# Moving the second softmax's transposes two slots earlier and rewriting TensorE's order in an attention and gated feed-forward kernel

## The chip, the cores and the metric

The kernel runs on one core of one Trainium2 chip. The metric is device time in microseconds. The times before are those of three runs; beside them stands one profiled execution, whose trace gives every duration in this document.

The engines go by the profile's names: PE is TensorE's matmul, PEld its weight load, DVE is VectorE, ACT is ScalarE, POOL is GpSimd, and SP is SyncE, which here only issues DMAs. SPq, POOLq and ACTq are the queues in which those engines issue DMAs, in program order.

## The reference

Four sequences x of 12416 rows by 128 go through an attention with 32 inducing points, and its result, 49664 rows by 128, through a gated feed-forward layer of width 1536:

```
def mab(q, kv):
    s = scale * (q @ kv.transpose(0, 2, 1))
    s = s - s.max(-1, keepdims=True)
    a = np.exp(s)
    a /= a.sum(-1, keepdims=True) + 1e-09
    return a @ kv
h = mab(I, x)                   # first softmax: 32 rows, each over 12416
y = mab(x, h)                   # second softmax: 12416 rows, each over 32
gate = 1.0 / (1.0 + np.exp(-(y @ w_gate)))
val = y @ w_val
out = gate * val @ w_out
```

## The kernel before

**The work.** A sequence is 97 chunks of 128 rows: six groups of 16 chunks and a single one. The attention result y is never formed. Since y = a2 h, the products h w_gate and h w_val (32 by 1536) are formed once for each sequence (tile `hwt`), and the feed-forward layer starts from the normalised weights a2 of the second softmax, transposed, in tiles `a2r`. A block is four chunks, 512 rows, by 12 slices of the width; a slice of a block is called a chunk of work below, as in the code. For each of them TensorE fills a gate bank (`g_ps`, 32 x 128 weights, 512 columns), ScalarE takes its tanh into a ring of 16 places (`issue_gate`, L1164), TensorE fills a value bank (`v_ps` or `vm_ps`, L1121), VectorE forms u = (tanh + 1) * v (`product`, L1351), and TensorE adds four 128 x 128 products of u with w_out into `acc_ps` (`out_mm`, L1250). After a block, ScalarE evacuates `acc_ps` into one of three buffers `o32` (L1275), and SP stores it (L1276).

**Beside it.** While the feed-forward layer of sequence b runs, the next sequence's first softmax (stage 1) and the second softmax of coming groups (stage 2) run in the gaps. `plan_stage2` lays out a group of stage 2: scores on TensorE (L651), copied by ScalarE (L688), row maxima by a tree on POOL (L698 to L703), the exponential on ScalarE (L712, the step called `weigh`), the row sums on POOL (L720 to L726), the reciprocal and the normalised weights `a2n` on POOL (L744 to L766), and last `turn`: SP issues a DMA that transposes `a2n` into one of three buffers `a2r` (L777). `plan_stage1` does the like for a group of the first softmax: scores (L368), a maximum on VectorE (L380), an exponential on ScalarE (L393), a transposing DMA on SP (`turn_dma`, L417), and sums on TensorE (L428). `x_transpose_dma` (L174) issues the transposes of x itself on SP.

**What sets the order.** The program writes each engine's instructions in one fixed order. Two things set it. The string `ORDER` is TensorE's order, written out by hand or by a planner beforehand: `g` fills a gate bank, `V` or `W` fills a value bank, `x` is VectorE's product, `o12` is twelve of the output products, and `p`, `a` and `d` let a waiting side step run on TensorE, ScalarE or VectorE. Value banks come in pairs, first `v2` with two chunks of work, then `vm` with one; after a `W` the second one has two as well, so a pair takes 3 or 4 chunks.

The second thing is the agenda. Every plan gives its steps a slot, and a slot is three chunks of work, counted from the beginning of the sequence (`position`); a sequence has 96. Before each fill of `v2`, `turn_page` takes the steps that have come due. A step marked "do" is issued at once, on whatever engine it uses; the others wait for their letter in `ORDER`. So the slot of `turn` decides where the transpose of `a2n` stands in SP's queue among the stores, the stage-1 transposes and the transposes of x. The exponential's slot is `weigh`, the sums come at weigh + 1, the normalising at weigh + 3, and `turn` at weigh + 8; it is weigh + 7 where the group takes the single chunk along (`far`), and weigh + 5 for the very first group (`soon`).

Of the kernel before, what the change touches and what calls it, by code (L numbers as in the profile page):

```python
# [54 lines left out]
NEXT = "the slot behind"  # L55
RING = 16
ORDER = """
ggVxgpgVxpVxgVd0xgo12gVxo8go4VxgVxgo12a0gVxgVxo12Vxa0gWxgo4Vxo4go4Vxgo8gVxo8gVxpgVxpo8a0gVxgVxo1
2a0gVxpVd0xgo12a0gWxo12gVxo4go4gWxo4Vxgo8go4a0gVxVxgpo8Vd0xgo12a0gVxo4gWxo4Vxgo8go4Wxgo4Vxo4a0gW
xgo12gVxo4go8gVxo4pa0gVxo4pa0gWxo8gVxo4gWxo4a0gVxgo12gVxo8pgVxpa0gVxo4Vxgo12gVxpgVd0xo12a1a0gVxg  # L60
o4Vxo12Wxgo4Vxgo4ggVxo4pgVxo4pgVxo4Vxa0go12Vxa0gpVd0xgo16a0gWxo8gVxo8go4gVxo4pgVd0xo8a1a0gVxgo4V
xo4po4gVd0xa0gVxo16gVxo4pgVxpo4a0gWxo12a0gVxVxgo12gVxo4ggVxpo4pVxa0go4gWxo12Vxgo4gVxo8pa0gVd0xa0
go8Wxo8gVxo8go4gVxo4pVxgo4pVxa0ggVxo12a0gVxgVxo4pVd0xgo4Vxgo20a0gVxo8pVxa0go4gVxo4pgVxo4pVxa0a0g
gVxo12Vxa0gpVxo4pa0gWxo4gVxo4go8gVd0xo8pVxgo8a0a0gWxgVxo12Wxa0go4go8gVxo8Wxgo4gVxo12a0gVxgo12gVx
o4gVxo4pgVxpo4a0gWxo8Vxgo4gWxo12a0gVxgo12gWxo4gVxo8go4gVxo8pVd0xggVd0xo4gVxo8a0gWxgo12Vxgo4Vxa0g
o12Vxgo8gVxo4Vxgo8a0gVxpVxgpo8a0gVxo8Vxgo4Wxgo8Vxgo8gVxo4gpa0gVxo4Wxo4a0ggVxo12Wxgo4Vxgo8gWxo4go
# [24 lines left out]
Vxo4gVxo8a0gVxpVxgo8pa0gVxo8gVxo4Vxgo4pVxa0go8Vxgo8gVxo4Wxo4Vxa0ggo12Wxgo4Vxgo8go4gVxo4pa0gVxo8g
Vxo4Vxo4a0gWxgo8gVxo16Wxa0go8gVxo4gVxo12a0gVxgo4Vxgo4pVxa0go4gWxo12Vxgo8Wxgo4gVxo12Vxa0ggo8pVxgo
4pVxa0go12Vxgo4Vxgo8pVxa0ggVxo8Vxo4a0gVxgo8Vxgo4Vxgo4gVxo8Vxgpa0gVxo16gWxo4Vxo4a0gVxgo16a0gVxo4g
Vxo8gVxo4gWxgo8Vxgo4Wxo4a0gVxgo12gVxo4go4pVxgo4pVxa0go8gVxo4VxggVxo12Vxa0gVxgo12Wxgo8Vxgo4go4Wxg
o8gVxo4Wxgo8a0gVxgo16Vxa0go4Vxgo12Vxgpa0gVxo8gWxo4gVxo4a0gWxgo12Vxgo4gWxo8go4gVxo8gVxo12pVxa0gpa
0gVxo8gVxo8Vxgpa0gVxo12Wxgo8gVxo12a0ggVxo12VxggVxo8pVxa0go4Wxgo12Vxgo8Wxgo4a0ggVxo12Wxga0gVxo8Vx
go12gpVxo4a0gVxo8gVxo4a0gVxgVxo12Vxgo8Vxgo4gVxpVxgo12a0gVxo8gVxo4a0gVxgVxo12gVxo8Vxgo4gVxpVxgo12
a0gVxo4gVxo8a0gVxgVxo12gVxo8Vxgpo4a0gVxo8Vxgo4gVxo4gVxo8a0gVxgVxo12gVxo8Vxgpo4a0gVxo8Vxgo4gVxo4V
xgo8a0ggVxVxpo12a0gVxo8Vxgo4gWxo4Vxgo4go4gWxo12a0ggVxo12gVxVxgo8pVxa0go4gVxo12gVxo4gVxo8a0gpVxgV
xo20a0gVxVxgpo12a0gVxo8Vxgo8Vxa0ggVxo12Vxgo4Vxgo8Vxgo4gVxo8gVxo4gVxo8a0gVxgo4Vxo4gVxpa0gVxo12gVx  # L100
o8gVxo4gVxo4Vxgo12a0ggVxVxo16Vxo4Vxo28
"""


# [1 line left out]
def kernel(  # L106
# [678 lines left out]
    def plan_stage2(at, b, c, score, take, weigh, far=None, soon=False):  # L785
        st = {}
        n = GC + (NLO if far is not None else 0)

        def room():
            st["sc"] = s2p.tile([P, GC + NLO, m], F32, tag="sc", name="sc", bufs=1)  # L790

        def one():
            room()
            st["s2"] = side_tile([P, GC, m], F32, "s2_ps")
            s2_score(b, 0, 0, NLO, st["s2"], True)

        def one_take():
            s2_take(st["sc"], GC, NLO, st["s2"])
            side_done()

        def half(j0, whole):
            if j0 == 0:
                st["s2"] = side_tile([P, GC, m], F32, "s2_ps")
            s2_score(b, c, j0, j0 + GC // 2, st["s2"], whole)

        def lower():
            if far is None:
                room()
            s2_take(st["sc"], 0, GC, st["s2"])
            side_done()  # L810

        def tree():
            s2_lower_pool(n, st["sc"])

        def most():
            st["hl"] = s2_max(GC, st["s2"])

        def exp():
            st["e"] = s2_exp(GC, st["s2"], *st["hl"]) if soon else s2_exp_low(n, st["sc"])
            if soon:  # L820
                side_done()

        def total():
            st["sme"] = s2_sum_pool(n, st["e"])

        def spread():
            rs = (s2_inverse if soon else s2_inverse_pool)(n, st["sme"])
            st["a2n"] = s2_spread(n, st["e"][:, 0:n, :], rs, nc.gpsimd)

        def turn():  # L830
            s2_turn_dma(b, c, GC, st["a2n"], "a2r")
            if far is not None:
# [20 lines left out]

# [590 lines left out]
```

## Time and profile before

| | us |
|---|---|
| median of three runs | 717.44 |
| lowest and highest of them | 716.08, 719.70 |
| the profiled execution's own time | 715.65 |
| its span, first to last instruction | 713.8 |

The span is what the trace covers; the 1.85 us beside it lie around the program. TensorE's granted clock was 0.999 of full speed on average. A page of the profile gives each engine's busy time, and the trace's views give the same by stretch, by group of like instructions, by wait and in order of time. In a group's row, the numbers after the first bar are the busy time of all its instructions and the mean of one in ns, and after the second bar the idle time of the engine just before them with what ended it. In a timeline row the first number is the start and the second the duration, both in us; a bracket holds the idle time before the instruction and what ended it.

### The profile page before, as it was taken

The numbers are of one execution on the slowest core, as the hardware profiler recorded it, in microseconds if no ns is written. First come the engines' busy times: TensorE is split into PE (matmuls) and PEld (weight loads), VectorE is DVE, ScalarE is ACT, GpSimd is POOL, SyncE is SP. The second block draws the span as 40 slices with busy tenths as digits, with TensorE's granted clock in tenths as the row PEclk, the third lists the DMA queues.
The fourth block names the chain that finished last, engine by engine and source line by source line (L and its number), as shares of the span: only waits on it lengthen the run. The fifth ranks groups of instructions, "written<-read, shape, count | busy, mean of one in ns | idle before, by whom it ended". The sixth has DMA issues, their size and how long they took to land.

```text
span 713.8 us, 21208 instructions
## 1 busy us (share of the span) xinstructions
PE 686.1 (96%) x8446; PEld 403.7 (57%) x8446; DVE 697.5 (98%) x780; ACT 677.3 (95%) x1019; POOL 445.8 (62%) x718
## 2 busy tenths in 40 slices
PE   8899999999999999999999999999999999999997
PEld 5455555655555655555555555555555555555555
DVE  6899999999999999999999999999999999999997
ACT  5699999999999999999999999999999999999996
POOL 4473764888663747588766266388767787666220
PEclk9999999999999999999999999999999999999999
DMA  9897494244478164335278530430323122023011
GB/s 212 126 175 148 86 174 116 75 91 107 89 124 173 55 129 96 56 76 126 62 121 151 110 75 31 90 75 32 77 61 61 60 62 76 30 76 76 30 47 46
DMA packets 118179, 65.74 MB, mean 92 GB/s; under 512 B 101408, under 2 KB 102208, under 8 KB 118080
## 3 DMA queue, kind: packets, MB, share of 16 engines
q1 hardware_dynamic: 112176, 50.90, 31.4%
q0 software_dynamic: 5584, 13.34, 11.0%
q8 instruction: 66, 1.08, 0.7%
q14 instruction: 33, 0.27, 0.1%
q10 hardware_dynamic: 320, 0.15, 0.1%
HBM read 27.80 MB, written 25.43 MB: 75 GB/s over the span
## 4 chain that ended last, share of the span: by engine, by line
PE 54%; ACT 18%; DVE 15%; issue 7%; POOL 2%; DMA 2%; DVEq 0%; ACTq 0%; POOLq 0%
PE acc_ps L1250 26%; DVE u L1351 14%; ACT t L1164 14%; PE g_ps L1121 13%; PE vm_ps L1121 5%; PE v_ps L1121 5%; ACT o L1275 3%; DMA xn<-in_x_dram 1%; PE vm_ps L651 1%; PE vm_ps L428 1%; DMA a2r<-a2n 1%; PE vm_ps L368 1%; POOL a2n L766 1%; DVE nm L380 0%; POOL near L744 0%
## 5 line engine op out<-in xcount | busy, mean ns | idle before, releaser
L1164 ACT ACTIVATE t<-g_ps 128x1024 f16<-128x1024 f32 (+1 forms) x770 | 588.6, 819 | 15.5 <-ACT t L1164 2.1
L1351 DVE SCALAR_TENSOR_TENSOR u<-t,v_ps 128x1024 f16<-128x1024 f16 x339 | 410.9, 1212 | 2.3 <-PE v_ps L1121 1.4
L1250 PE MATMUL acc_ps<-wo,u 128*128 128x128 f16 x4596 | 366.5, 220 | 5.4 <-ACT o L1275 0.3
L1250 PEld LDWEIGHTS <-u 128*128 128x128 f16 x4620 | 263.5, 98 | 155.7 <-issue 146.7
L1351 DVE SCALAR_TENSOR_TENSOR u<-t,vm_ps 128x512 f16<-128x512 f16 (+1 forms) x340 | 303.5, 893 | 0.6 <-PE vm_ps L1121 0.4
L1121 PE MATMUL g_ps<-a2r,hwt 32*128 32x512 f16 (+1 forms) x1179 | 286.3, 375 | 5.5 <-DMA a2r<-a2n 1.3
L1121 PEld LDWEIGHTS <-hwt 32*128 32x128 f16 x2382 | 99.5, 91 | 112.8 <-issue 38.5
L1121 PE MATMUL v_ps<-a2r,hwt 32*128 32x512 f16 (+1 forms) x694 | 130.5, 373 | 4.7 <-DVE u L1351 2.8
L1121 PE MATMUL vm_ps<-a2r,hwt 32*128 32x512 f16 (+1 forms) x485 | 129.8, 376 | 2.3 <-DVE u L1351 1.5
L720 POOL TENSOR_TENSOR sum<-e 128x256 f32<-128x256 f16 (+1 forms) x23 | 15.4, 671 | 130.7 <-ACT e L712 127.2
L766 POOL TENSOR_TENSOR a2n<-e,rs 128x2048 f16<-128x2048 f16 (+3 forms) x25 | 86.8, 3474 | 4.5 <-DVE rs L738 2.8
L744 POOL TENSOR_TENSOR near<-sme,minus 128x16 f32<-128x16 f32 (+1 forms) x22 | 65.2, 2966 | 1.7
L1275 ACT ACTIVATE o<-acc_ps 128x512 f32<-128x512 f32 x96 | 57.8, 602 | 0.2
L699 POOL TENSOR_SCALAR rise<-rise 128x256 f32<-128x256 f32 (+6 forms) x110 | 51.2, 466 | 9.7
L700 POOL TENSOR_TENSOR top<-top,rise 128x128 f32<-128x128 f32 (+3 forms) x88 | 28.4, 323 | 7.3
L720 POOL TENSOR_TENSOR sum<-sum 128x128 f32<-128x128 f32 (+3 forms) x92 | 28.4, 309 | 7.2
L698 POOL TENSOR_TENSOR rise<-top 128x128 f32<-128x128 f32 (+3 forms) x88 | 27.3, 310 | 6.9
L698 POOL TENSOR_TENSOR rise<-sc 128x256 f32<-128x256 f32 (+1 forms) x22 | 16.2, 737 | 18.8 <-ACT sc L688 18.6
L1220 POOL TENSOR_TENSOR xn_spare<-xn_spare 128x512 f16<-128x512 f32 x9 | 11.4, 1269 | 22.2 <-ACT xn_spare L1218 22.0
L703 POOL TENSOR_TENSOR sc<-sc,top 128x512 f32<-128x512 f32 (+1 forms) x22 | 23.9, 1086 | 1.7
L1215 POOL TENSOR_SCALAR xn_spare<-xn_spare 128x512 f32<-128x512 f16 x9 | 13.4, 1492 | 18.1 <-ACT xn_spare L1213 18.1
L651 PEld LDWEIGHTS <-xT 128*128 128x128 f16 x388 | 14.0, 96 | 7.6 <-issue 6.9
(165 smaller groups left out, 331.3 us busy)
## 6 DMA issues: line engine op xcount, KB each, us to landing
out_dram<-o SPq DMA_DIRECT2D x96, 256.0 KB, 2.1
xn<-in_x_dram POOLq DMA_DIRECT2D x18, 512.0 KB, 6.8
xn<-in_x_dram POOLq DMA_DIRECT2D x3, 544.0 KB, 6.4
xn<-in_x_dram POOLq DMA_DIRECT2D x3, 256.0 KB, 11.7
xn<-in_x_dram SPq DMA_DIRECT2D x1, 576.0 KB, 4.7
xn<-in_x_dram SPq DMA_DIRECT2D x1, 512.0 KB, 3.8
a2r<-a2n SPq DMA_TRANSPOSE x29, 4.4
wg<-in_moe_w_gate_dram POOLq DMA_DIRECT2D x1, 384.0 KB, 12.6
```

Source lines behind the costliest of these rows:

```text
L698: nc.gpsimd.tensor_tensor(out=r, in0=far, in1=near, op=ALU.subtract)
L699: nc.gpsimd.tensor_scalar_max(out=r, in0=r, scalar1=0.0)
L700: nc.gpsimd.tensor_tensor(out=top[:, 0:n, 0:w], in0=near, in1=r, op=ALU.add)
L703: nc.gpsimd.tensor_tensor(out=sc[:, 0:n, :], in0=sc[:, 0:n, :], in1=top[:, 0:n, 0:1].to_broadcast((P, n, m)), op=ALU.subtract,)
L720: nc.gpsimd.tensor_tensor(out=d[:, 0:n, :], in0=src[:, :, 0:w], in1=src[:, :, w : 2 * w], op=ALU.add)
L744: nc.gpsimd.tensor_tensor(out=near[:, 0:n], in0=sme[:, 0:n], in1=minus1[:, 0:n], op=ALU.pow)
L766: eng.tensor_tensor(out=a2n[:, 0:n, :, :], in0=e.unsqueeze(2).to_broadcast((P, n, 4, m)), in1=rs.unsqueeze(2).unsqueeze(3).to_broadcast((P ...
L1121: made_mm.append(nc.tensor.matmul(out[:, col : col + nb * P], hw[b][r : r + 32, j // 2, :], a2r[r : r + 32, o : o + nb, :].rearrange("p j ...
L1164: i = nc.scalar.activation(out=ring[:, p : p + n, :], in_=g[:, 0:n, :], func=AF.Tanh, scale=0.5)
L1250: mm = nc.tensor.matmul(acc[0][half][:, i, :], u[:, ts(i, P)], wo16[:, j, :], start=(i in fresh), stop=not left[ib] and not any(e[1] == ib ...
L1275: nc.scalar.mul(out=o32[:], in_=bank_[:], mul=0.5)
L1351: x = nc.vector.scalar_tensor_tensor(out=u[:, 0:n, a:e], in0=ring[:, p : p + n, a:e], scalar=1.0, in1=v[:, 0:n, a:e], op0=ALU.add, op1=ALU ...
```

## The change

The slot of `turn` goes from weigh + 8 (or + 7) to weigh + 6, and for the very first group from weigh + 5 to weigh + 4. `ORDER` is replaced as a whole; the first and the last lines are shown. No instruction's form changes, and the functions that read the string are the same.

```diff
 ORDER = """
-ggVxgpgVxpVxgVd0xgo12gVxo8go4VxgVxgo12a0gVxgVxo12Vxa0gWxgo4Vxo4go4Vxgo8gVxo8gVxpgVxpo8a0gVxgVxo1
...
-xgo8a0ggVxVxpo12a0gVxo8Vxgo4gWxo4Vxgo4go4gWxo12a0ggVxo12gVxVxgo8pVxa0go4gVxo12gVxo4gVxo8a0gpVxgV
-xo20a0gVxVxgpo12a0gVxo8Vxgo8Vxa0ggVxo12Vxgo4Vxgo8Vxgo4gVxo8gVxo4gVxo8a0gVxgo4Vxo4gVxpa0gVxo12gVx
-o8gVxo4gVxo4Vxgo12a0ggVxVxo16Vxo4Vxo28
+ggVxgVxpgpVxgo4gVd0xo4Vxgo12Vxgo4ggVxo12a0gVxgWxo12Vxa0ggWxo12Vxgo4go4Vxgo4gVxo4gVxpo4pVxa0go4Wx
...
+4VxgVxgo8Vxgo4Vxgo12Vxa0gpa0gVxo20gVxVxpgo12a0gVxo4gVxo12Vxa0gVxgo12VxgpVxa0go12Vxgo8gVxo4VxgVxg
+o12Vxa0gVxgo12VxgVxgo12gVxo4gVxo8gVxo4Vxgo8a0gVxgo8VxgVxpa0gVxo12gVxo4Vxgo8gVxo4Vxgo12Vxa0ggVxo1
+6VxVxo32
 """
@@ plan_stage2
             (weigh + 1, "do", total, 2700),
             (weigh + 3, "do", spread, 3700 if soon else 7600),
-            (weigh + (5 if soon else 8 if far is None else 7), "do", turn, 0),
+            (weigh + (4 if soon else 6), "do", turn, 0),
             needs=[(heads[b], 7)] if b else (),
```

In letters, the old string has 770 g, 540 V, 138 W, 678 x and 631 runs of o, and the new one 770 g, 535 V, 141 W, 676 x and 617 runs of o. Both hold 4656 output products, 140 p, 214 a and 34 d.

More of the change, by code (lines that the diff above doesn't have):

```diff
@@ L99 @@
-xgo8a0ggVxVxpo12a0gVxo8Vxgo4gWxo4Vxgo4go4gWxo12a0ggVxo12gVxVxgo8pVxa0go4gVxo12gVxo4gVxo8a0gpVxgV
-xo20a0gVxVxgpo12a0gVxo8Vxgo8Vxa0ggVxo12Vxgo4Vxgo8Vxgo4gVxo8gVxo4gVxo8a0gVxgo4Vxo4gVxpa0gVxo12gVx
-o8gVxo4gVxo4Vxgo12a0ggVxVxo16Vxo4Vxo28
+ggVxgVxpgpVxgo4gVd0xo4Vxgo12Vxgo4ggVxo12a0gVxgWxo12Vxa0ggWxo12Vxgo4go4Vxgo4gVxo4gVxpo4pVxa0go4Wx
+go12Vxa0gVxgo12gpVd0xgo8a0gWxo12gVxo4gWxo4gVxo8a0ggVxo12gVxpgVd0xo4Vxgo12a0ggWxo8gVxo12Vxa0ggVxo
+12Vxa0go4pgVxo4pVxa0go4gVxo8gVxo4gVxo12Wxa0gVxgo12gVxo4go4pVxgpa0gWxo12Vxgo4gVxo12Vxa0gpgo8Vd0xV
@@ new lines @@
+xgo8a0go4gWxo4Vxgo4Vxgo4gpVxgo4pVxa0ggVxo12a0gVxpgVd0xo16a0gWxo16gVxo4gVxgo4pVd0xgo4Vxo4a0a0gpVd
+0xgo8Wxa0go12gVxo8gVxo8gpVxpa0gVxgVxo12Vxa0ggVxo12gVxpgVxpo8a0gWxo8gVxo8gVxo12pVd0xa0ga0go12Wxo4
+gVxo4go8gVxo4pgVxo4pVxa0ggVxo12a0gVxgVxpo8gVd0xa0gVxo20gVxpo8a0gVxo4gVxpVxgpo8a0a0gWxgVxo12Vxa0g
+o8pVxgpa0gWxo4Vxgo4ggVd0xo8pa0gVxo12Wxa0ggVxo20Wxggo8gVxo8gWxo12a1gVxgo8gVxo4pgVxpo4a1a0gWxo12gV
+xo8gWxo4gVxo8a0gVxgo8Vxgo8gWxo8Vxgo4go4gVxo8gVxo8Vxa0gVxgo8gVxo8a0gVxo8Vxgo8gVxo4VxgpgVd0xo12Vd0
+xa0gVxgo12gVxpgVxo8pa0gVxo4Vxgo12Vxgpa0gVxo12a0gVxVxgo8Wxgo8Vxgo8gWxo4go4gVxo4gWxgo12Vxa0gWxgo8g
@@ new lines @@
+Vxo8gWxgo4a0gVxo12gVxo16pVxa0a0ggWxo12gVxo4gVxo8go4gVxo4gWxo4Vxgo12a0gWxgo8Vxgo8gVxo8pgVxpo4a0gW
+xo4Vxgo4gWxo12a0ggVxo8gWxo8Vxgo8go4gWxo8gVxo4gWxo8a0gVxgo16Wxa0go4gVxo8go4WxggVxo8gWxo8a0gVxgo8W
+xgo8go4gVxo8gWxo8gVxo4go8Vxa0gpVxgo4pVxgo8a0gVxo4gWxo8Vxgo8gVxo4gpVd0xgo12a1a0ggWxo8Vxo8gVxo4gVx
+o4ggWxo8gVxo4gVxo12Vxa0ggpo8Vd0xVxgo8a0go8gVxpo4pa0gVxo4Wxgo8Vxgo8a0ggWxo8Vxgo8gVxo4pa0gVxpo4a0g
+Wxo8gVxo8gWxo8a0ggVxo12gVxo4pgVxpo4a0gWxo8Vxgo8gVxo12Vxa0gpgo8Vd0xVxgo12a0ggVxo8gVxo4gWxo4Vxgo4g
+o8a0gVxpgVd0xo12a0gWxo4gVxo8gVxo8gpVxgo4pVxgo4a0gVxo8Vxpa0gVd0xgo12Vxgo12a1a0gVxo4Vxgpo8gVd0xo4g
@@ new lines @@
+Vxpo8pa0a0gVxgWxo12gVxo4gVxo8gpVxpa0gWxgo8Vxgo8gVxo8Vxpa0gVd0xgo8Vxa0go12gWxo4gVxo4ggVxo8Vxgo12p
+a0gVd0xVxo4a0go8Vxgpa0gVxo12gVxppVxa0go8Wxgo4gVxo12a0gWxgo8Vxgo16Vxa0go4pVxgo4pVxa0go8Vxgo8a0gVd
+0xpa0gVxo12gWxo8gVxo4go4Wxgo4gVxo8gWxo8a1gVxgo12gVxo4pgVxpo4a1gVxo4Vxgo8a0gWxo8Vxgo8Wxa0ggo12Vxg
+o4Wxgo8gVxo8gVxgo8Vxgo8a0gVxgVxo12Vxa0go4gVxo8Vxgo4gVxo4pgVd0xo4gVd0xo12Vxa0gpo4Vxgpo4a0gWxo8gVx
+o4gWxo8go4gVxo8gVxo8pa0a0ggVxo4Wxo8gVxo8Vxgo4go8gVxo4gWxo12Vxa0ggWxo8go4Vxgo4Wxgo8gVxgo8a0gVxo8p
+a0gVxo8a0gWxVxgo12Wxgo8gVxo4go4gWxo8gVxo12a0gWxgo8Vxgo8gVxgpVxpa0gWxo4Vxgo8gWxo4go4gVxo8gWxo4a0g
@@ new lines @@
+gVxo16gWxo8Vxgo4go4gVxo4gVxo12Wxa0gVxgo20Wxa0ggo8gVxo8gWxo12a0gVxgo8Wxgo8gVxo4gWxo4ggVxo8gWxo16V
+xa0ggo8gVxo4pgVxo4pVxa0go4Vxgo8gWxo8gVxo8gVxo4a0gpVd0xgo12a0gWxo8gVxo4Wxgo4go8gVxo12a0gVxgpVd0xo
+12a0gWxo4gVxo4go4gVxo4pVxgpo4a0gWxo8Vxgo8a0ggWxo12Vxgo8Vxa0go4pVxgpo4a0gWxo8gVxo12a0gWxgo4Vxgo8g
+Vxo8pgVxpo4a0gVxgVxo12gVxo4Vxgo8pa0gVd0xa0gVxo16gWxo4gVxo4go8gWxo4gVxo8go4a0gVxpVd0xgo12a0gWxo8V
+xgo4gVxo8gpVxgo4pVxgo4a0gVxo8Vxpa0gVd0xgo12Vxgo12a1a0gVxo4Vxgo8pgVd0xo4gVxpo8pVxa0a0ggWxo12gVxo4
+gVxo8gpVxpa0gWxgo8Vxgo8gVxo8Vxa0gpgo4Vd0xVxa0go16gWxo4Vxgo4go4gVxo8gVxpo8a0gVd0xVxo4a0go12gVxpVx
@@ new lines @@
+a0go12gVxpVxgo8pa0gWxgVxo12a0gWxgo12Vxgo4Vxa0go12pgVxo4pVxa0go4Vxgo12a0gVd0xpa0go4Vxo4gWxo4gVxo8
+gWxgo12gVxo8gWxo8a1ggVxo8Vxgo8pgVxpo4a1gVxo4Vxgo8a0gWxo4gVxo12a0gWxgo12Vxgo4gWxo8gVxo8gVxgo8gVxo
+8a0gVxgVxo12Vxa0go4gVxo8Vxgo4Vxgpo4gVd0xo4gVd0xo12Vxa0gpo4Vxgpo4a0gWxo8Vxgo4gWxo8go4gVxo8gVxo8pa
+0a0ggVxo4Vxo8gVxo4gWxo4Vxgo4go8gWxo4gVxo4gWxo8a0gVxgo8Wxa0go12Vxgo12gVxo4go4pa0gVxo4Wxo4Vxa0ggo1
+2Wxgo8Vxgo4go4gWxo8gVxo4gWxo8a0ggVxo16gVxo4pgVxpo4a0gWxo8gVxo4gWxo12a0gVxgo12Wxgo4Vxgo4go8gWxo4g
+Vxo8gWxo8a0gVxgo16Vxa0ggo4Vxo4gVxpo4a0gVxo8gWxo12a0gVxgWxo8gVxo4go8gWxo4Vxgo4gVxgo8Vxgo12Vxa0gpV
@@ new lines @@
+xgo8pVxgo8a0gVxo4Vxgpo4a0gVxo8Vxgo8Vxgo4Wxo4Vxa0ggo12gWxo4Vxgo4go8gVxo8pVxa0go4gVxo4Vxo4a0gWxgo1
+2Vxgo12Vxa0go4Vxgo8gWxo4gVxo8a0gVxgo12pa0gVxo4gVxo12VxggWxo8Vxgo8gWxo4a0ggVxo16gVxo4pgVxpo4a0gVx
+o4Vxgo8pVxa0go4Vxo8a0gVxgVxo8gVxgo4gVxo8gVxpa0gVxo16gWxo12Vxa0gVxgo20a0gVxgVxo8gVxo4gWxgo8Vxgo4W
+xo4a0gVxgo12gVxo4go4pVxgpa0gVxo12gVxo4Wxgo12Vxa0gWxgo12gVxo4go4Wxgo8go4Vxgo4Wxgo8Vxgo4a0ggWxo12g
+Vxo8gWxo8a0gVxgo20Vxa0gpa0gVxo8Vxgo4Vxgo8gWxo4gVxo4go4gVxo8gVxo8Vxa0gpgVxpo8a0gVxo12Vxgo4Vxgpo8a
+0gVxo4Vxgo12a0gVxgVxo12VxgVxgo8pa0gVxo4Wxgo12Vxgo4gWxo8a0ggVxo8Wxga0gVxo12gVxo12gpVxo4a0gVxgVxo1
@@ L102 @@
+2a0gVxgVxo12Vxgo8gVxo4gVxpa0gVxo12gVxo4Vxgo8a0gVxgVxo12gVxo8gVxo4gVxo4gVxpo4a0ggVxo16a0gVxgWxo12
+Vxgo8gVxo4gVxpo8a0gWxo4gVxo12a0gVxgo8gVxo8gVxpa0gVxo12gVxo4Vxgo4gVxgVxo12a0gVxpa0gVxo12gVxo8gVxo
+4VxgVxgo8Vxgo4Vxgo12Vxa0gpa0gVxo20gVxVxpgo12a0gVxo4gVxo12Vxa0gVxgo12VxgpVxa0go12Vxgo8gVxo4VxgVxg
+o12Vxa0gVxgo12VxgVxgo12gVxo4gVxo8gVxo4Vxgo8a0gVxgo8VxgVxpa0gVxo12gVxo4Vxgo8gVxo4Vxgo12Vxa0ggVxo1
+6VxVxo32
 """
```

40 lines of the change are left out of this document (removed).

## The prediction, as it was put on record

> **What bounds the kernel now.** I read the page's busy shares first, then the table of busy time by stretch, then the groups by shape, then VectorE's own waits.
>
> ```profile
> span 713.8 us, 21208 instructions
> PE 686.1 (96%) x8446; PEld 403.7 (57%) x8446; DVE 697.5 (98%) x780; ACT 677.3 (95%) x1019; POOL 445.8 (62%) x718
> ```
>
> Three engines stand at 95% or more of the whole span, so the shares alone do not say which one sets the pace. The table by stretch does (in each row: length, then PE, PEld, DVE, ACT and POOL busy time):
>
> ```profile
> 36.00:40.00 4.00, 3.54 (x38) 1.68 (x35) 3.61 (x5) 3.59 (x6) 2.15 (x6) 1.00 0.49 90
> 40.00:710.00 670.00, 651.23 (x8018) 384.67 (x8016) 667.26 (x704) 652.01 (x971) 426.79 (x676) 1.00 0.41 88
> ```
>
> In the 670.00 us that hold nearly all of the feed-forward part, VectorE works 667.26 us. It is idle for 2.74 us, while TensorE is idle for 18.77 us and ScalarE for 17.99 us. VectorE is therefore the bound, and its work comes from three groups, the products u = (t + 1) * v:
>
> ```profile
> L1351 DVE SCALAR_TENSOR_TENSOR u<-t,v_ps 128x1024 f16<-128x1024 f16 x339 | 410.9, 1212 | 2.3 <-PE v_ps L1121 1.4 <-ACT t L1164 0.3 <-issue 0.2
> L1351 DVE SCALAR_TENSOR_TENSOR u<-t,vm_ps 128x1024 f16<-128x1024 f16 x138 | 167.2, 1212 | 0.1
> L1351 DVE SCALAR_TENSOR_TENSOR u<-t,vm_ps 128x512 f16<-128x512 f16 x200 | 135.5, 678 | 0.5 <-PE vm_ps L1121 0.4
> ```
>
> Of the 2.74 us, VectorE's own waits between 40 and 710 us name only these:
>
> ```profile
> DVE u L1351 <- PE v_ps L1121: 1.4, 3, 0.8
> DVE o L1267 <- PE vm_ps L1250: 0.4, 1, 0.4
> DVE u L1351 <- issue: 0.2, 1, 0.2
> ```
>
> One wait of 0.8 us is the largest, and the timeline shows that the change touches its cause:
>
> ```profile
> 404.36 0.62 ACT L712 ACTIVATE e<-sc 128x512 f16<-128x512 f32 x1
> 411.61 3.61 POOL L766 TENSOR_TENSOR a2n<-e,rs 128x2048 f16<-128x2048 f16 x1
> 416.78 1.20 SPq L417 DMA_TRANSPOSE a<-a1T  x1
> 418.10 2.74 SPq L777 DMA_TRANSPOSE a2r<-a2n  x1
> 424.03 0.39 PE L1121 MATMUL g_ps<-a2r,hwt 32*128 32x512 f16 x2 [1.33 <-DMA a2r<-a2n]
> 424.50 1.22 DVE L1351 SCALAR_TENSOR_TENSOR u<-t,v_ps 128x1024 f16<-128x1024 f16 x1 [0.80 <-PE v_ps L1121]
> ```
>
> POOL had the normalised weights a2n ready at 411.61 + 3.61 = 415.22. SyncE sent their transpose only at 418.10, because a stage-1 transpose (L417) stood ahead of it in SP's queue and could not go before 416.78. The chain that ended last goes through that transfer, which took 5.89 us to land, at about 424.0:
>
> ```profile
> 418.10 5.89 DMA a2r<-a2n
> ```
>
> TensorE then stood 1.33 us, and VectorE 0.80 us.
>
> **The change part by part.** *The words of the order.* Counting the letters of both strings: g 770 and 770, V 540 and 535, W 138 and 141, x 678 and 676, o-runs 631 and 617 (4656 o either way). With W a pair takes 4 chunks instead of 3, so products of two chunks go from 477 to 479 and products of one from 201 to 197 (the profile's 200 plus the last, cut in two). What a product occupies on VectorE is read from consecutive starts, since neighbours overlap:
>
> ```profile
> 690.85 0.68 DVE L1351 SCALAR_TENSOR_TENSOR u<-t,vm_ps 128x512 f16<-128x512 f16 x1
> 691.45 1.21 DVE L1351 SCALAR_TENSOR_TENSOR u<-t,v_ps 128x1024 f16<-128x1024 f16 x1
> 692.58 0.68 DVE L1351 SCALAR_TENSOR_TENSOR u<-t,vm_ps 128x512 f16<-128x512 f16 x1
> ```
>
> One chunk takes 0.60 us and two take 1.13. The change is -4 x 0.60 + 2 x 1.13 = **-0.14 us**. By the full durations (678 and 1212 ns) it would be -0.29; I take the starts. ScalarE's and the other engines' instruction counts stay as they are.
>
> *The moved transposes.* A slot is three chunks. The first product and the last two pieces give its length:
>
> ```profile
> 29.76 1.22 DVE L1351 SCALAR_TENSOR_TENSOR u<-t,v_ps 128x1024 f16<-128x1024 f16 x1 [0.27 <-ACT t L1164]
> 708.53 0.74 DVE L1351 SCALAR_TENSOR_TENSOR u<-t,vm_ps 128x384 f16<-128x384 f16 x2
> ```
>
> (709.27 - 29.76) / 1155 chunks = 0.588 us a chunk, 1.765 us a slot. Two slots earlier is 3.5 us, one slot 1.8. In the group above, batch 2, slot 24 is 29.76 + (576 + 72) x 0.588 = 410.8; a2n ends at 415.22. So SP will now wait up to 4.4 us for POOL with the transpose at its head, and send it at 415.2 instead of 418.1: 2.9 us earlier, landing near 421. TensorE's wait was 1.33, so it goes with 1.5 us to spare, and VectorE gets **-0.80 us** back. What is late next is nothing on this path: the landing then leads its reader by that 1.5 us. In the other groups no such wait shows, so the earlier transfer is worth nothing there.
>
> What is queued behind the waiting transpose on SP is three things. First, the stage-1 transpose L417: in batches 0 to 2 its score slots 24 and 40 are the very slots to which the a2 transposes of groups 2 and 3 move, so these now go ahead of it. In batch 2 L777 leaves SP at 415.22 + 2.74 = 417.96, and L417 goes 1.2 us later than 416.78. Its reader is far off:
>
> ```profile
> 427.09 0.24 PE L428 MATMUL vm_ps<-xn,a 128*32 128x128 f16 x4
> ```
>
> Second, the stores of the output. The longest wait will be that of a group whose POOL work was delayed:
>
> ```profile
> 120.42 14.10 SPq L1276 DMA_DIRECT2D out_dram<-o  x3
> 132.74 3.61 POOL L766 TENSOR_TENSOR a2n<-e,rs 128x2048 f16<-128x2048 f16 x1
> 136.38 1.86 SPq L777 DMA_TRANSPOSE a2r<-a2n  x1
> ```
>
> Its slot was 58 (29.76 + 174 x 0.588 = 132.1) and becomes 56 (128.6); a2n is ready at 136.35 either way, so SP stands 7.8 us instead of 4.3. Stores come every 7 us (three starts within 14.1) and o32 has three buffers, so one store late by 8 us is covered; without the third buffer ScalarE's o would wait. Third, the first group's move from slot 8 to 7 puts its transpose ahead of the x transpose due at slot 7:
>
> ```profile
> 42.12 3.61 POOL L766 TENSOR_TENSOR a2n<-e,rs 128x2048 f16<-128x2048 f16 x1 [0.89 <-DVE rs L738]
> 45.32 3.41 SPq L174 DMA_TRANSPOSE xT<-xn  x1
> 48.83 1.95 SPq L777 DMA_TRANSPOSE a2r<-a2n  x1
> 54.59 0.40 PE L368 MATMUL vm_ps<-xT,indT 128*32 128x512 f16 x4
> ```
>
> That one goes from 45.32 to 45.73 + 1.95 = 47.7, so 2.4 us later; its reader is at 54.59. All three cost 0; together their cover is gone if a reader comes 2 to 5 us sooner than now.
>
> *TensorE's redrawn order.* Each run of o begins with a stall of the weight loads:
>
> ```profile
> PEld L1250 <- issue: 147.6, 592, 0.8
> ```
>
> That is 0.249 us a run. Fourteen runs fewer spare TensorE 3.5 us, hidden entirely: TensorE has 18.77 us of slack and VectorE none. The waits that the new order makes for VectorE are not to be read from this trace. Bounds: below, all idle time left over goes, 2.74 - 0.80 = 1.94 us gained; above, a late refill in one pair of products out of ten. The size of such a lateness I take from TensorE's own waits on VectorE, 0.2 us each:
>
> ```profile
> PE v_ps L1121 <- DVE u L1351: 2.5, 11, 0.3
> ```
>
> 338 pairs / 10 x 0.2 = 6.8 us lost. I take 0, because the strings resemble each other where it matters: fills preceded by 16 or more o number 24 before and 23 after, and tanh leads of at most one chunk at a fill number 63 before and 46 after, which is a little safer.
>
> *The end.* The old string closes V x o4 V x o28, the new one V x V x o32, so four o move behind the last fill:
>
> ```profile
> 707.61 0.39 PE L1121 MATMUL vm_ps<-a2r,hwt 32*128 32x128 f16 x4
> 707.93 1.57 PEld L1250 LDWEIGHTS <-u 128*128 128x128 f16 x28
> ```
>
> 1.57 / 28 = 0.056 us each, and nothing covers them: 4 x 0.056 = **+0.22 us**. Both strings put seven products ahead of the first exponential, so the start counts 0, with the 4.00 - 3.61 = 0.39 us of idle time there as what could be gained.
>
> **Sum:** -0.14 - 0.80 + 0.22 = -0.72 us. The profiled execution took 715.65 us (span 713.8, 1.85 around it), so it would become 714.9. It lies 1.79 us under the median of the three runs, 717.44, and I apply the difference there: **716.7 us**.
>
> **Rivals.** *Nothing comes of it (717.4).* The landing at 424 could stay late if the earlier transpose meets other transfers, or the redrawn order could ask for the group sooner. Then -0.14 + 0.22 remains. For it: SP waits for POOL anyway. Against it: the 2.9 us lay in SP's queue, not in POOL.
>
> *The redrawn order fits worse (723).* The v2 bank is single, so it must be refilled while VectorE works on the other product, 0.60 us in a narrow pair. A TensorE run that ends too late stalls VectorE each time. It decides from 0.5%, 3.6 us, that is 3.6 / 338 = 11 ns a pair, or 0.2 us in one pair of nineteen. At one in ten: 717.44 - 0.72 + 6.8 = 723.5. For it: with 2.74 us of idle time in 670 almost any other order has more to lose than to win. Against it: the counts above.
>
> *SP's queue strikes back (722).* Transposes that wait for POOL hold up L417 in six places (slots 24 and 40 of three batches). If each made a sum late as at 424, 0.80 us: 6 x 0.80 = 4.8, with -0.14 + 0.22, gives 722.3. It decides once L417 lands after its sum, that is over 5 us later than now; the row at 427.09 speaks against it. [...]
>
> *TensorE was the bound after all (713.2).* Then the fourteen runs are worth 3.5 us, and -3.5 - 0.72 gives 713.2. VectorE's 99.6% speaks against it. [...]
>
> **How the numbers follow.** Chances: forecast 0.52, nothing 0.14, worse order 0.21, SP's queue 0.07, TensorE 0.06. About 0.5% (3.6 us) is what a measurement of this kernel tells from no change; the three runs shown span 716.08 to 719.7. Within: 0.66; slower: 0.28; faster: 0.06. VectorE's own limit is 717.44 - 0.14 - 2.74 = 714.6; with the runs' spread below the median (1.36) halved, the range begins at 713.9. At the top it takes in SP's queue and half of the worse-order case (one pair in thirteen: 5.2 us), 722.0.
>
> **What would show it.** Right: no TensorE wait on a2r near 424; L777 ahead of L417 on SP and within 0.1 us of a2n's end; VectorE idle 1.5 to 3 us in the 670; 479 and 197 products. Wrong: VectorE's waits on v_ps or vm_ps above 5 us in many pieces (worse order); waits of TensorE on a or xT (SP's queue); a time down by more than 3 us with VectorE's idle time unchanged, which would make my bound wrong.

## The result, and the profile after

| | before | after |
|---|---|---|
| median of 21 runs each, us | 717.44 | 715.24 |
| lowest and highest, us | 715.95, 721.02 | 715.06, 718.01 |

The ratio is 0.997, with a 95% interval from 0.9956 to 0.9985: the kernel became 0.3% faster, which is clear of the noise but within the 0.5% that the prediction counts as no change. The median fell by 2.20 us where 0.72 was forecast.

The runs of either kernel fall into two groups with a gap between them. Of before's 21, ten lie from 715.95 to 716.49 and eleven at 717.44 or more; of after's, eighteen lie from 715.06 to 715.49 and three at 716.58, 716.80 and 718.01. So the lower group moved by about 0.9 us (716.1 to 715.2), and fewer executions fall into the upper one. These are two effects, and they are taken apart below. The profiles of both kernels are of executions in the lower group; that of before, 715.65 us, stands 0.45 us under the group's middle.

First comes the top of the page of after:

```profile
span 713.3 us, 21230 instructions
PE 685.7 (96%) x8446; PEld 403.4 (57%) x8446; DVE 697.5 (98%) x778; ACT 678.3 (95%) x1019; POOL 445.8 (62%) x718
```

The span fell by 0.5 us only, because the first product came later in this execution; between executions of any of these kernels it came anywhere from 29.76 to 31.14 us. So the table of busy time by stretch is read from the start of the first product to the end of the last. This is the row of before, and then that of after (length, then PE, PEld, DVE, ACT and POOL busy, then the granted clock):

```profile
29.76:709.27 679.51, 660.26 (x8117) 389.46 (x8117) 676.81 (x714) 661.35 (x983) 432.13 (x685) 1.00 0.41 89
```

```profile
30.17:708.76 678.59, 660.38 (x8117) 389.12 (x8117) 676.73 (x712) 662.40 (x983) 432.12 (x685) 1.00 0.41 89
```

The stretch became 0.92 us shorter. VectorE's work fell by 676.81 - 676.73 = 0.08 us, and its idle time from 2.70 to 1.86, so by 0.84. VectorE is still the bound. Its groups by shape in after show the words of the new string:

```profile
L1351 DVE SCALAR_TENSOR_TENSOR u<-t,v_ps 128x1024 f16<-128x1024 f16 x338 | 409.7, 1212 | 1.1 <-ACT t L1164 0.3 <-PE v_ps L1121 0.2 <-PE g_ps L1121 0.2
...
L1351 DVE SCALAR_TENSOR_TENSOR u<-t,vm_ps 128x1024 f16<-128x1024 f16 x141 | 170.9, 1212 | 0.0
L1351 DVE SCALAR_TENSOR_TENSOR u<-t,vm_ps 128x512 f16<-128x512 f16 x196 | 132.9, 678 | 1.0 <-PE vm_ps L1121 0.4 <-ACT t L1164 0.3 <-ACT o L1275 0.2
```

338 + 141 = 479 products of two chunks, and 196 of one beside the last, which is cut in two. The idle time that went is that of the first row: 2.3 us there before, of it 1.4 for v_ps, and now 1.1, of it 0.2. VectorE's waits between 40 and 710 us no longer hold one above 0.4 us:

```profile
DVE o L1267 <- PE vm_ps L1250: 0.4, 1, 0.4
DVE u L1351 <- ACT t L1164: 0.3, 1, 0.3
DVE u L1351 <- PE v_ps L1121: 0.2, 1, 0.2
```

The timeline of after at the place of the old wait:

```profile
410.23 3.61 POOL L766 TENSOR_TENSOR a2n<-e,rs 128x2048 f16<-128x2048 f16 x1
413.87 1.69 SPq L777 DMA_TRANSPOSE a2r<-a2n  x1
416.92 1.22 SPq L417 DMA_TRANSPOSE a<-a1T  x1
423.04 0.39 PE L1121 MATMUL g_ps<-a2r,hwt 32*128 32x512 f16 x2
423.81 1.21 DVE L1351 SCALAR_TENSOR_TENSOR u<-t,v_ps 128x1024 f16<-128x1024 f16 x1
426.26 0.24 PE L428 MATMUL vm_ps<-xn,a 128*32 128x128 f16 x4
```

The transpose (L777) now leaves 0.03 us after a2n is done (410.23 + 3.61 = 413.84), and L417 follows it where it had led. The transfer itself, from issue to landing, is in the trace's rows of the tile:

```profile
DMA to landing us min/median/max: 4.4/4.4/4.4
```

It landed at 413.87 + 4.4 = 418.3, 4.7 us ahead of its reader at 423.04, which has no bracket: it waited for nothing. L417's reader at 426.26 has none either.

The time that SP stands waiting for POOL shows in its own waits between 40 and 710 us, first of before, then of after:

```profile
SPq L777 <- POOL rise L699: 31.0, 6, 8.5
```

```profile
SPq L777 <- POOL rise L699: 70.2, 9, 9.4
SPq L777 <- POOL a2n L766: 35.1, 6, 7.9
```

All waits of L777 in that time come to about 80 us before and 169 after, and the longest of after is 10.2 us. They cost nothing: the waits of after in that time hold no row for a transposing DMA. The stores, which stand in the same queue, waited 412.0 us for ScalarE's `o` (L1275) before and 309.0 after, so a part of SP's waiting only changed its place.

At the end of the program, the timeline of after:

```profile
707.21 1.79 PEld L1250 LDWEIGHTS <-u 128*128 128x128 f16 x32
708.02 0.74 DVE L1351 SCALAR_TENSOR_TENSOR u<-t,vm_ps 128x384 f16<-128x384 f16 x2
```

The last run of o now has 32 products and begins 708.76 - 707.21 = 1.55 us ahead of the last product's end; before it had 28 and began 709.27 - 707.93 = 1.34 ahead. It begins 0.21 us earlier and is 0.22 longer. From the last product to the end of the span there were 4.53 us before and 4.54 after.

### The profile page after: what moved, and what is told of

It reads as the page before. It is cut to its first block, busy times and chain, and to the rows that moved or that the text cites. A ratio compares the mean times of both kernels' runs of the same rounds, so it can differ in the third digit from the quotient of the medians.

```text
span 713.3 us, 21230 instructions
## 1 busy us (share of the span) xinstructions
PE 685.7 (96%) x8446; PEld 403.4 (57%) x8446; DVE 697.5 (98%) x778; ACT 678.3 (95%) x1019; POOL 445.8 (62%) x718
## 4 chain that ended last, share of the span: by engine, by line
PE 52%; DVE 19%; ACT 17%; issue 9%; DMA 1%; POOL 1%; DVEq 0%; ACTq 0%; POOLq 0%
PE acc_ps L1250 25%; DVE u L1351 17%; PE g_ps L1121 13%; ACT t L1164 13%; PE vm_ps L1121 5%; PE v_ps L1121 4%; ACT o L1275 3%; DMA xn<-in_x_dram 1%; PE vm_ps L651 1%; PE vm_ps L428 1%; ACT a1T L393 0%; DVE nm L380 0%; PE vm_ps L368 0%; ACT sc L688 0%; PE vm_ps L1203 0%
## 5 line engine op out<-in xcount | busy, mean ns | idle before, releaser
L1250 PE MATMUL acc_ps<-wo,u 128*128 128x128 f16 x4596 | 364.8, 220 | 4.7 <-ACT o L1275 0.5
L1250 PEld LDWEIGHTS <-u 128*128 128x128 f16 x4620 | 263.2, 98 | 151.5 <-issue 143.5
L1275 ACT ACTIVATE o<-acc_ps 128x512 f32<-128x512 f32 x96 | 57.7, 601 | 0.4 <-PE acc_ps L1250 0.2
L1220 POOL TENSOR_TENSOR xn_spare<-xn_spare 128x512 f16<-128x512 f32 x9 | 11.4, 1272 | 22.0 <-ACT xn_spare L1218 21.9
```

The lines of the kernel that those rows point to most:

```text
L1250: mm = nc.tensor.matmul(acc[0][half][:, i, :], u[:, ts(i, P)], wo16[:, j, :], start=(i in fresh), stop=not left[ib] and not any(e[1] == ib ...
L1275: nc.scalar.mul(out=o32[:], in_=bank_[:], mul=0.5)
```

## The experiments

The theory: a wait for a2r near 424 us, made by SP's queue, was all that the change removed. Its first rival gave the gain to the redrawn order; its second said that the transposes were late whatever stood ahead of them. A question came up on the way: what puts executions into the upper group. Every time here is a median, with the lowest and highest run behind it; the ratio is that to runs of the kernel before on the same chip, with its 95% interval (before's medians: 716.57 beside the slots alone, the one group alone and the first order-only kernel; 716.63 beside one slot less, three more, the second order-only kernel and the changed kernel again; 717.49 beside the denser and the sparser piece; 716.51 beside the empty and the second denser one). "The stretch took" gives the time from the first product to the end of the last in the profiled execution. An execution counts as upper at 716.5 us or more, and for before, whose lower group stands higher, above 717 us.

**The slots alone.** The old string, with the new slots:

```diff
-            (weigh + (5 if soon else 8 if far is None else 7), "do", turn, 0),
+            (weigh + (4 if soon else 6), "do", turn, 0),
```

> The old written order with the new slots (6 and 4). SP theory: the wait of TensorE at 424 us is gone, VectorE's wait of 0.80 with it, and the time is 715.0 to 715.8; the spread of the kernel before (values near 716.1 and near 717.6) shrinks to one value. Order theory: as before, 716.1 to 717.6. Third theory (transposes at the head of SP's queue cost as much as they save): 717 or more, with TensorE waiting for a or xT.

Measured: 715.37 us (714.94 to 717.99), ratio 0.9968 [0.9939, 0.9997]. The stretch took 678.63 us, as with the whole change (678.59), and no wait for a2r is left. The slots carry all of the gain.

**One group's slot alone.** The old string, and only the group whose exponential stands at slot 18 moved, the third one of the first three sequences:

```diff
+            (weigh + (5 if soon else 6 if weigh == 18 else 8 if far is None else 7), "do", turn, 0),
```

> The old written order; only the groups whose weights stand at slot 18 (the third group of sequences 0 to 2) are transposed 6 slots behind them, the others stay at 8, 7 and 5. If one group's late landing in each sequence is the whole gain of the slots, this gives the same time as all slots moved (within 0.3 us). If the other groups' moves matter too, it lies between the kernel before and that one.

Measured: 715.40 us (714.84 to 715.96), ratio 0.9964 [0.994, 0.9989]; the stretch took 678.58 us. SP's timeline in this kernel:

```profile
416.13 1.70 SPq L777 DMA_TRANSPOSE a2r<-a2n  x1
...
419.21 1.22 SPq L417 DMA_TRANSPOSE a<-a1T  x1
```

This one group of each sequence suffices; the other moves of the slots are worth nothing that can be measured.

**One slot less, and three more.** The same with 7, then with 11, in place of 6:

```diff
+            (weigh + (5 if soon else 7 if weigh == 18 else 8 if far is None else 7), "do", turn, 0),
```

> The old written order, the groups at slot 18 transposed 7 slots behind their weights. In sequence 2 this puts the transpose just ahead of the stage-1 transpose in SP's queue, one slot (1.8 us) earlier than before instead of two. Queue theory (what counts is to stand ahead of the stage-1 transpose; POOL's end decides when it goes): the whole gain, the same time as with 6 slots within 0.3 us, and no wait near 424. If the slot itself counted: about half of the gain, and a wait of 0.3 to 0.8 us left.

Measured: 715.55 us (714.84 to 717.95), ratio 0.9982 [0.9966, 0.9998]; the stretch took 678.73 us. The timeline of this kernel shows why one slot does what two do:

```profile
411.87 3.61 POOL L766 TENSOR_TENSOR a2n<-e,rs 128x2048 f16<-128x2048 f16 x1
415.51 1.33 SPq L777 DMA_TRANSPOSE a2r<-a2n  x1
417.04 1.83 SPq L417 DMA_TRANSPOSE a<-a1T  x1
```

One slot earlier already puts L777 ahead of L417, and from there POOL sets its start (411.87 + 3.61 = 415.48). Even with the 5.89 us of before it would have landed at 421.4, ahead of the 422.70 (424.03 - 1.33) at which TensorE was ready in before. What counts is the place in the queue, not the distance.

> The old written order, the groups at slot 18 transposed 11 slots behind their weights, the suspected wait made larger: in sequence 1 the transpose goes behind one more store (about 253.1 us instead of 249.0), in sequence 2 it keeps its place. Late-landing theory: two waits of TensorE for a2r, about 3 us near 255 and 1.3 us near 424, VectorE loses 3 to 4 us instead of 0.8, the time is 719 to 721, and the stretches behind the waits show a lower granted clock in more of the executions. If the landing did not matter: 716.2 to 717.5, as before.

With 11 the median was 727.87 us (725.43 to 733.02), ratio 1.0166 [1.0137, 1.0194]. The direction was as expected and the size was missed. The profiled execution was the longest of six; its timeline in an earlier sequence:

```profile
245.21 3.61 POOL L766 TENSOR_TENSOR a2n<-e,rs 128x2048 f16<-128x2048 f16 x1
...
256.49 8.76 SPq L777 DMA_TRANSPOSE a2r<-a2n  x1
257.33 1.18 POOL L165 DMA_DIRECT2D xn<-in_x_dram  x2
...
267.70 0.61 PE L1121 MATMUL g_ps<-a2r,hwt 32*128 32x512 f16 x2 [10.13 <-DMA a2r<-a2n]
...
269.88 1.22 DVE L1351 SCALAR_TENSOR_TENSOR u<-t,vm_ps 128x1024 f16<-128x1024 f16 x1 [10.95 <-PE g_ps L1121]
```

The transpose held SP for 8.76 us, where 1.3 to 2.8 us are seen for the group at 424 us in the other kernels, and landed only when TensorE went on, 11.2 us after its issue. Two loads of x were issued 0.84 us behind it. No run took them away, but the profiles of before and after show the like: five transposes there left 0.08 to 0.09 us behind a load of x (at 182.55 and 352.85 us before, at 104.23, 183.67 and 353.07 after) and took 7.5 to 9.9 us to land, and the others of whole groups took 3.6 to 6.7. VectorE lost 10.95 us in this one wait, twice the 5.3 us (three slots of 1.765) by which the slot was moved. The rest of the excess goes with the clock: it averaged 0.51 of full speed from 262 to 276 us, and it stood at 0.50 again from 440 to 443 us, in the next sequence; TensorE's two waits for a2r come to 11.4 us here, so the second took about 1.3. All six runs show a mean clock of 0.995 or less, as the theory expected.

**The redrawn order alone**, with the old slots, on two chips:

```diff
-            (weigh + (4 if soon else 6), "do", turn, 0),
+            (weigh + (5 if soon else 8 if far is None else 7), "do", turn, 0),
```

> The new written order with the old slots (8, 7 and 5 behind the weights). SP theory (the gain of 2.2 us comes from the transposes that no longer stand behind stage-1 transposes in SP's queue): the gain is gone, 716.5 to 717.5, and TensorE waits for a2r near 424 us or at a like place. Order theory (the gain comes from the redrawn words of TensorE): 715.0 to 715.5, as the changed kernel, with no such wait.

> The new written order with the old slots once more, beside the changed kernel. Its first profile had no wait for a2r, but a stretch at a lower clock near 93 to 96 us. Theory of two sufficient parts (either the slots or the new order alone takes the late landing away): the same time as the changed kernel within 0.3 us, and 678.6 us from the first product to the end of the last in an execution without such a stretch. Theory that the slots alone bring the gain: 0.5 to 1 us above it, with a wait for a2r.

Measured: 715.85 us (715.17 to 717.78), ratio 0.9973 [0.9947, 0.9999], and on the other chip 715.97 (715.72 to 717.31), ratio 0.9987 [0.9977, 0.9997]. The result lies between the theories: this order too has no wait for a2r, although its transpose still stands behind L417. SP's timeline of the first of the two:

```profile
418.67 1.20 SPq L417 DMA_TRANSPOSE a<-a1T  x1
419.99 1.96 SPq L777 DMA_TRANSPOSE a2r<-a2n  x1
```

and the reader in the same kernel:

```profile
425.31 0.39 PE L1121 MATMUL g_ps<-a2r,hwt 32*128 32x512 f16 x2
```

and the transfer:

```profile
DMA to landing us min/median/max: 4.3/4.3/4.3
```

It landed at 424.3, 1.0 us ahead of the reader. Before, the transpose left 424.03 - 1.33 - 418.10 = 4.6 us ahead of the moment at which TensorE could have used it and took 5.89; here it leaves 5.3 us ahead and takes 4.3. With the 4.3 to 4.4 us that this transfer took without the wait (4.3 in both profiles of order-only, 4.4 in the changed kernel and with one group's slot alone), before's would have landed between 422.4 and 422.5, while TensorE could have used it at 422.70. So the wait had two parts: the late place in the queue, and a transfer longer by 1.5 to 1.6 us. It took 5.9 us in both profiles of before; why it is longer there stays open. The two halves of the change are two cures for one wait, and together they give no more than the slots alone. The order alone gives less: it stands 0.48 us above the slots alone on the first chip and 0.34 above the whole change on the second (715.63). Both its profiles show VectorE idle for 0.3 us in front of a product that nothing in the profile held up; in the changed kernel the longest such wait is of 0.2 us. Why stays open. Both profiles of order-only are of executions in the upper group, so its lower one was not seen in a trace.

**The changed kernel again**, unaltered, on the chip of the one-slot and order-only-again kernels:

> The changed kernel, unchanged, on the same chip as the others of this set, as their yardstick. From its first profile: 678.6 us from the first product to the end of the last, no wait for a2r, a time near 715.2. If the redrawn order adds something of its own to the slots, it stands at least 0.3 us under the kernels that move slots alone; if not, it is within 0.3 us of them.

Measured: 715.63 us (714.97 to 717.59), ratio 0.998 [0.9964, 0.9996]. It lies within 0.1 us of the one-slot kernel on the same chip, so the redrawn order adds nothing measurable to the slots. The profile fell on an upper execution, 717.59. Its stretch took 680.15 us, 1.56 more than in the first profile of the same kernel. There is no wait for a2r in it; what differs is the clock (the third number from the end), and that opened the second question:

```profile
92.00:94.00 2.00, 1.94 (x17) 1.15 (x17) 2.00 (x4) 2.00 (x5) 0.00 (x0) 0.76 1.10 213
94.00:96.00 2.00, 2.00 (x20) 1.37 (x19) 1.33 (x2) 1.39 (x3) 0.93 (x2) 0.50 1.30 117
96.00:98.00 2.00, 2.00 (x26) 1.13 (x25) 1.37 (x2) 1.36 (x2) 1.59 (x6) 0.88 1.26 296
```

**The kernel before again**, unaltered, one profile:

> The kernel before, unchanged, for a second profile. Its 21 runs cluster near 716.1 and near 717.6. If this execution falls near 717.6, its trace shows where 1.5 us go: by the SP theory in longer waits of TensorE for a2r (over 1.33 us, or in more than one place); by a rival, that the start varies (the loads of x), in a later first product than 29.76 us. If it falls near 716.1 it should repeat the first profile's single wait of 1.3 us.

Measured: 717.38 us, an upper execution. The stretch took 681.00 us against 679.51 in the first profile, 1.49 more. The timeline has the same wait as the first profile:

```profile
424.32 0.60 PE L1121 MATMUL g_ps<-a2r,hwt 32*128 32x512 f16 x2 [1.35 <-DMA a2r<-a2n]
...
425.02 1.22 DVE L1351 SCALAR_TENSOR_TENSOR u<-t,v_ps 128x1024 f16<-128x1024 f16 x1 [1.04 <-PE v_ps L1121]
```

but the table by stretch shows what came behind it:

```profile
423.00:424.00 1.00, 0.00 (x0) 0.00 (x0) 0.97 (x2) 1.00 (x2) 1.00 (x1) 1.00 0.64 238
424.00:425.00 1.00, 0.68 (x6) 0.25 (x7) 0.00 (x0) 0.13 (x2) 0.02 (x1) 0.64 0.01 4
425.00:426.00 1.00, 1.00 (x11) 0.74 (x9) 0.98 (x1) 1.00 (x1) 0.00 (x0) 0.50 0.63 129
426.00:427.00 1.00, 1.00 (x10) 0.63 (x8) 0.73 (x2) 0.46 (x1) 0.00 (x0) 0.50 0.02 2
427.00:428.00 1.00, 1.00 (x12) 0.44 (x10) 0.77 (x2) 0.16 (x2) 0.00 (x0) 0.66 0.00 0
428.00:429.00 1.00, 1.00 (x25) 0.55 (x22) 1.00 (x1) 1.00 (x2) 0.00 (x0) 1.00 0.00 0
```

TensorE's clock fell to half right behind the wait. It lacked 0.36 + 0.50 + 0.50 + 0.34 = 1.70 us of full clock, which at half speed is 3.40 us; in finer slices, of 0.42 or 0.43 us, it stands at 0.50 in all eight from 424.28 to 427.68 us, and in no other from 32 us on below 0.99. From 425 us on TensorE is busy in every slice, and VectorE, the bound elsewhere, stands for 0.02 + 0.27 + 0.23 us in the first three of them beside its 1.04. The product ahead of the wait starts at 423.03 us in the first profile and at 423.30 in this one, and the last product ends at 709.27 and 711.00: 1.46 of the 1.49 us are lost in between. That the upper group of before is made of such falls is borne out by the clocks and by the counts. For 103 of its 124 runs over all chips each run's mean clock is known: of the 47 above 717 us 46 show 0.997 or less, and of the 56 others 55 show 0.999 or more. Over all chips 58 of the 124 lie above 717 us, and with the wait gone and the old string kept (slots alone, one group, one slot) 2 of 35 lie above 716.5. One fall of this size makes a mean of 0.997 or 0.998, and about half of the 46 stand at 0.997. The others go down to 0.981, at 725.32 us, and so lack more of the clock than one such fall; no execution of this kind was profiled. Of before's runs 17 lie above 719 us, and none of the 91 of the changed kernel, of order-only and of the kernels that only move the slots to 6 or 7. In the first profile of before, the same wait left the clock alone:

```profile
424.00:425.00 1.00, 0.97 (x15) 0.64 (x15) 0.49 (x1) 0.54 (x1) 0.00 (x0) 1.00 0.00 0
```

So half clock followed a wait of 1.35 us in one execution, and did not follow one of 1.33 us in another; what decides between the two no run shows.

**The place where the changed kernel's clock falls.** In the three upper executions of the changed order that were profiled, the clock fell between 92 and 98 us. In one of them, the first of order-only, TensorE's matmuls show no wait from 86 to 95 us, and in all three TensorE is busy for 1.89 us or more of every 2 from 88 to 96. There the string has short runs of o between many gate and value fills. Three kernels change only this piece, with the same 48 products in it, and the slots stay as changed. More products in the stretch:

```diff
-o16a0gWxo16gVxo4gVxgo4pVd0xgo4Vxo4a0a0g
+o12a0gWxo8gVxo8gVxgo8pVd0xgo8Vxo4a0a0g
```

> The changed kernel with 16 output products moved into the stretch ahead of the lower clock (88 to 92 us, where only four runs of four o stood). Theory that a stretch with few output products on TensorE lets its clock fall: no lower clock at 93 to 96 us, and no execution 1.4 to 2 us above the others (3 of 21, then 2 of 12, stood so with the changed kernel). Theory that the fall has nothing to do with the words: one to three of 12 executions 1.4 us or more above the others, and the same row at a lower clock in a profile that catches one. The rest at 715.2 to 715.8, or 0.2 to 0.4 more where the longer runs of o delay a refill.

Measured: 715.43 us (714.89 to 715.77), ratio 0.9969 [0.9951, 0.9986]. None of 12 runs lies in the upper group.

Fewer:

```diff
-o16a0gWxo16gVxo4gVxgo4pVd0xgo4Vxo4a0a0g
+o20a0gWxo16gVxgVxgo4pVd0xgVxo8a0a0g
```

> The changed kernel with output products moved out of the same stretch, so that about 3 us hold only four of them. Theory that a stretch with few output products lets the clock fall: the granted clock falls in most executions at about 92 us, their times stand 1.4 to 2 us higher, the median is 716.5 to 717.5. Theory that the fall has nothing to do with the words: one to three of 12 executions, as before, and a median of 715.2 to 715.8.

Measured: 715.99 us (715.25 to 718.82), ratio 0.9976 [0.9952, 1.0]. Four of 12 lie at 716.5 or more: the direction is right, but it is fewer than expected. Three of the four stand at 718.4 to 718.8 with a mean clock of 0.995, so they lose more than one fall. Its table by stretch, in a profile of the upper group, against that of after:

```profile
90.00:92.00 2.00, 1.50 (x18) 0.74 (x16) 2.00 (x4) 1.83 (x4) 0.00 (x0) 1.00 1.09 253
92.00:94.00 2.00, 1.90 (x16) 0.99 (x13) 1.39 (x3) 2.00 (x4) 0.00 (x0) 0.54 1.28 185
94.00:96.00 2.00, 2.00 (x24) 1.51 (x22) 1.31 (x2) 0.91 (x3) 1.41 (x3) 0.61 1.15 186
```

```profile
90.00:92.00 2.00, 1.93 (x17) 0.88 (x16) 2.00 (x4) 1.95 (x5) 0.00 (x0) 1.00 1.11 254
92.00:94.00 2.00, 1.94 (x30) 1.35 (x27) 2.00 (x4) 2.00 (x5) 0.00 (x0) 1.00 1.26 185
94.00:96.00 2.00, 2.00 (x41) 1.29 (x37) 2.00 (x3) 1.83 (x4) 1.68 (x4) 1.00 1.22 166
```

The clock lacks 0.92 + 0.78 = 1.70 us again, which by an estimate is 3.40 us, if it stood at 0.50 as in the second profile of before, and VectorE stands for 0.61 + 0.69 = 1.30 us in two slices that it fills in after.

None in most of the stretch:

```diff
-o16a0gWxo16gVxo4gVxgo4pVd0xgo4Vxo4a0a0g
+o20a0gWxo16gVxgVxgpVd0xgVxo12a0a0g
```

> The changed kernel with no output product at all from about 88 to 91 us; they follow in a run of twelve. Theory that a stretch with few output products lets the clock fall: at least 8 of 12 executions 1.4 us or more above the lowest ones, and a lower granted clock at about 92 us in the profile (with four products in the stretch it was 4 of 12, with sixteen 2 of 12 and 3 of 21, with twenty-eight 0 of 12). Theory that the words do not matter: 1 to 3 of 12.

Measured: 717.36 us (715.40 to 718.76), ratio 1.0009 [0.9997, 1.0022]. Seven of 11 lie in the upper group: the median went there, and with it the whole gain of the change. The one profile is of the fastest run, at full clock, so where the clock falls in the others was not seen. The denser one was run beside it:

> The kernel with the denser stretch once more, for the count: by the theory that few output products let the clock fall, again no execution 1.4 us or more above the others, so 0 of about 24; if the words do not matter, 2 to 6 of 24, at the rate of the changed kernel (9 of 56 in its order).

Measured: 715.38 us (714.65 to 716.26), ratio 0.9981 [0.9971, 0.9991]; none of 11 lies in the upper group.

Counting runs at 716.5 us or more: none of 23 with the dense piece, 9 of 56 with the changed order as it is (both halves and order-only), 4 of 12 with the sparse one, 7 of 11 with the empty one. On one chip the dense and the empty piece stand at none of 11 and 7 of 11, on another the dense and the sparse one at none of 12 and 4 of 12. The eleven upper runs of the sparse and the empty piece have a mean clock of 0.994 to 0.998, and their twelve others 0.999 or 1.0. So the make-up of this stretch changes how often the clock falls; the step from the changed order to the dense piece alone is too small to show it by itself. With fewer products TensorE also idles more (1.50 us busy of 2.00 in the sparse kernel's first row, 1.93 in after), so the count of products and the small gaps are not told apart. Why it falls in one execution and not in the next of the same kernel stays open.

No version beats the changed kernel by more than can be measured: slots-only, one group, one slot and denser have medians from 715.37 to 715.55, the changed kernel 715.24 and 715.63. The denser one has the fewest upper executions.

## Why the prediction was right or wrong

The time, 715.24, lies inside the range and within 0.5% of before, the likeliest case; the forecast was 1.5 us too high.

- **The bound and the main term held.** VectorE's idle time was to fall by 0.80 us and fell by 0.84. The wait went, and it went by the place in SP's queue, as one group's move of one slot shows. The landing was earlier than I wrote: 4.7 us to spare, not 1.5, because the transfer took 4.4 us instead of 5.89 and a2n was ready 1.4 us sooner. That 5.89 was itself a part of the wait I had not counted: I put all of it down to the queue.
- **The words:** -0.14 forecast, -0.08 measured, in the direction of the count.
- **The tail was wrong:** +0.22 forecast, 0.0 measured. I counted four products more at the end and let them begin when the old run did. But the o4 that stood between the last two fills is gone, so the run itself begins 0.21 us earlier.
- **The sum** for an undisturbed execution, -0.72, is -0.92 by the stretch and about -0.9 by the lower groups of runs.
- **The step that failed** is the last: "It lies 1.79 us under the median of the three runs, 717.44, and I apply the difference there". The 1.79 were not a constant around the program. Some 1.3 of them lie between the lower group's middle (716.1) and the median, and by the profile and the clocks above this is the fall of the clock behind the very wait that the change removes, which the one profiled execution had happened to escape. The other 0.45 is that execution's place at the low end of its group. In the one upper execution of before that was profiled, the wait cost 1.49 us more than in the first profile. The median sat in the upper group and came down into the lower one: 0.9 for the stretch, and the other 1.3 of the 2.20 for that.
- The size of this second part depends on where before's median happens to fall. Beside the changed kernel again, 13 of 29 runs of before lay above 717, its median was 716.63, and the difference was 1.00 us. That the median fell by three times the forecast is in this sense chance.
- **The rivals.** "Nothing comes of it" fell with the wait. "The redrawn order fits worse" was wrong as I described it, since VectorE's other idle time did not grow (1.90 us before, 1.86 after); what the order does have is a thin stretch near 90 us, which costs about 1.5 us in some executions, with the clock at 0.50 behind it (1.56 us in the one profiled for the changed kernel). "SP's queue strikes back" was wrong: L777's waits doubled, the longest was 10.2 us where I wrote 7.8, and no reader was late. "TensorE was the bound" was wrong: before, its weight loads at L1250 spent 146.7 us in issue stalls by the groups' view (147.6 by the waits' view, from which the prediction took it), and in after

```profile
L1250 PEld LDWEIGHTS <-u 128*128 128x128 f16 x4620 | 263.2, 98 | 151.5 <-issue 143.5 <-DVE u L1351 2.9
```

they spend 143.5 (144.2 by the waits' view, in 579 stalls instead of 592). These 3.2 to 3.4 us, where 3.5 were forecast, left no mark on the time.

## What to carry to other kernels

When a transfer lands late, look first at what stands ahead of it in its queue: moving one group's issue ahead of one other here did all that the change of all slots and of 4656 products' order did (the stretch took 678.58 and 678.59 us). Look also at how long the transfer itself takes, since here the wait needed both, the place in the queue and 5.89 us instead of 4.3 to 4.4. When runs of one kernel fall into two groups, profile one of each and compare the granted clock by stretch, before carrying a difference from one profile over to a median. A wait on TensorE, here of 1.35 us, or a stretch with few products and small gaps can cost more than its own length if the clock falls behind it: here 1.49 and 1.56 us more.

## What the hardware showed unexpectedly

- TensorE's clock fell to 0.50 for 3.40 us behind a wait of 1.35 us, and in the changed kernel it stood at 0.50 from 93.20 to 96.17 us, where TensorE had been busy for 1.90 us or more of every 2 from 88 us on. Each of the two falls cost the program about 1.5 us (1.49 in the kernel before, 1.56 in the changed one). In the kernel with three slots more, with a wait of 10.13 us, it stood at 0.51 on average from 262 to 276 us.
- A transposing DMA of the same size took 4.3 to 5.9 us to land in the group at 424 us, and 11.2 us in an earlier sequence, where two loads of x were issued 0.84 us behind it; it held its queue for 1.3 to 2.8 us, and for 8.76 there. Right behind a load of x, five others took 7.5 to 9.9 us.
